# A layernorm, linear-attention and gated-MLP kernel: 96 bytes less padding, and another order of the opening

## The chip, the cores and the metric

The kernel runs on one core of a Trainium2 chip. A core has five engines that work side by side, each with its own queue of instructions in order: TensorE (PE, matrix products into PSUM), VectorE (DVE, elementwise work and reductions), ScalarE (ACT, copies and activation functions), GpSimd (POOL, elementwise work on SBUF) and SyncE (SP, which here issues nearly all DMAs). SBUF is the working memory of 128 partitions, PSUM the eight banks of 128 x 512 float32 into which PE writes. The metric is the time of one execution on the device in microseconds (us).

## The reference

All inputs are float32. `x` is 2048 x 1024.

```python
xn = layernorm(x)                       # over the 1024 columns, eps 1e-5
q, k, v = split_heads(xn @ wqkv)        # 32 heads of 32
phi(t) = concat(softmax(t @ w_phi), softmax(-(t @ w_phi)))      # per head
num = phi(q) @ (phi(k)^T @ v);  den = phi(q) @ sum(phi(k)) + 1e-6
s = merge_heads(num / den) @ wo
g = silu( (silu(xn @ w1) * (xn @ w3)) @ w2 )                    # w1, w3: 1024 x 3584
out = x + s * g
```

## The kernel before

**Products.** Each float32 operand is split into two float32r parts, a rounded one ("hi", a cast on ACT) and the rest ("lo", a subtraction on DVE). A product of two operands takes three passes of matmuls: hi x hi, hi x lo, lo x hi. On top of that the large products use Strassen's scheme with seven products of half size: A's halves give A11, A12, S1, S2, S3, S4, A22, the weights' halves B11, B21, T1, T2, T3, B22, T4. What the text calls *a product* is one of these seven for one block: 4 x 3 = 12 matmuls of 128 x 128 (stationary) by 128 x 512 (moving) into one PSUM bank (`products`, L703). Bank `a` takes A12; bank `c` S1, then S4; a bank `b` (four of them) A11, then S2, S3 and A22 on top. `out_of` (`evict`) takes the sum out of the bank behind each product; the next one that adds to the same bank waits for that.

**Stages.** (1) Layernorm of x and the transposes of it. (2) Gate and up (w1, w3): 2 halves of x (`tb`) x 28 column blocks x 7 products = 392 products of L703; the stationary operand is a weight block `bo` (a tile of the pool `q`), the moving one a tile `op0...` (first half of x) or, behind *the turn*, `op1...` (second half). (3) k, v and q (L927): 3 passes over 8 pairs of row tiles, 7 products each; stationary `xo...` (pool `q`), moving the weight tiles `op2...`, `op3...`, `op4...`. (4) w2 (L1333): 7 x 8 rounds of 7 blocks of 6 matmuls; stationary `af`/`as`, moving `bo` from a ring of 24 tiles (`ring`: 8 of pool `ra`, 12 of `rb`, 4 of `rw`). (5) The attention output times wo (L1460), stationary `oT` (pool `q`), moving `wos` (the same ring).

**Where tiles lie.** Pools are stacked from the left end of a partition (`edge_l`, `misc`, `small`, `work`, `q`, `big`; later `acc` and `rb` in the place of `big`) and from the right end (`edge_r`, `rw`, `bdp`, `xp`; later `spare` and then `ra` in the place of `bdp` and `xp`). `edge_l`, `edge_r` and the tile `pad` in `small` hold nothing; their sizes shift what is stacked behind them. `op0...` tiles are all in `big`. Of `op1...`, A11 and A12 are in `spare`; of `op2...`, T2 and T1; of `op3...`, T3 and B22; of `op4...` none (`HOMES`). In this program `small` ends at byte 5216 of the partition, 96 past a multiple of 512; all sizes behind it up to `big` are multiples of 512, so all these tiles start 96 past one. `big` ends at 179,296, `spare` starts at 179,712 = 351 x 512, and every tile of the right side but the edge starts on a multiple of 512.

**The opening.** Everything up to the 14th product is written out by hand, and each engine keeps that order. Tiles x0 to x3 are normalized, turned (`turn`: four transposes on PE into a PSUM tile `pt` of the tag `tr`, two buffers), copied out (`raw_x`, ACT) and cast (`hi`, ACT): one such pair of ACT instructions is *a piece*; there are four for A11 and four for A12. Tiles x4 to x7 follow (`nm_scalar` is the shift and scale on ACT; `other_turns`, two turns each, A22's, copied out by ACT, and A21's, read by DVE in `first_sums`, which makes S1 and S3). The sums S2 (`second_sums`) and S4 (`last_sums`) are DVE's. `b_first` to `b_third` make the weights' sums on POOL; `hold_sums` is a small copy on POOL that keeps it back until a given tile is written. `finish_h0` is a SiLU on ACT, for blocks 2 and 3 with a store to `hs_d`.

**Folds.** 32 weight blocks of q and k are multiplied by the block diagonal of w_phi (`fold`, eight PE instructions for one, into `tr`), copied back (`copy_fold`, ACT) and stored. Six of them are done in the opening (`load_fold` loads two into one `q` tile), the other 26 in the main loop (`side_fold`), every sixth step from the main loop's first on.

Of the kernel before, what the change touches and what calls it, by code (L numbers as in the profile page):

```python
# [8 lines left out]
F = mybir.dt.float32  # L9
# [8 lines left out]
P = 128  # L18
# [3 lines left out]
G = 8  # L22
NKB = NF // 4
EPS = 1e-5
PAD = 32


@with_exitstack
def tile_kernel(ctx: ExitStack, tc: tile.TileContext, x, wkT, wqT, wv, wphi, wo, w1, w3, w2, out):
# [3 lines left out]
    def pool(name, bufs, **kw):  # L33

        open_pools[name] = tc.tile_pool(name=name, bufs=bufs, reuse_waits="tile", **kw)
        return open_pools[name].__enter__()
# [108 lines left out]
    ps = pool("ps2", 2, space=PSUM)  # L145
    BANKS = {"a": 1, "b": 4, "c": 1}
# [7 lines left out]
    def slot(m, j):  # L154
        name = f"op{m}" + (ANAMES if m < 2 else BNAMES)[j]
        j = HOMES[m][j]
        if j < 7:
            return big.tile([P, 2, 4, 512], R, name=name, tag=f"big{j}")
        return spare.tile([P, 2, 4, 512], R, name=name, tag=f"spare{j}")
# [12 lines left out]
    def quad(name, dt=R):  # L172
        return qp.tile([P, 2, 4, P], dt, name=name, tag="q")

    def blk(name):
        return xp.tile([P, 4, P], F, name=name, tag="x")

    def flat(t):
        return t.rearrange("p k t -> p (k t)")
# [3 lines left out]
    eps_t = consts[:, 0:1]  # L183
    small.tile([P, PAD], F, name="pad", bufs=1)
    bd = bdp.tile([P, G, P], F, name="bd")
# [32 lines left out]
        for a in range(2):  # L218
            nc.vector.tensor_scalar(xt[a], xt[a], mv[:, j, 0:1], sd[:, 1, j:j + 1], op0=OP.subtract, op1=OP.mult)

    def turn(half):
        pt = ps.tile([P, 4, P], F, name="pt", tag="tr", bufs=2)
        for k in range(4):
            nc.tensor.transpose(pt[:, k, :], half[:, k * P:(k + 1) * P], ident)  # L224
        return pt

    def raw_x(pt):
        xf = blk("xf")
        nc.scalar.copy(xf, pt)
        return xf  # L230
# [13 lines left out]
    def load_w(wT, dch, c, t=None):  # L244
        wr = blk("wr") if t is None else t
        nc.sync.dma_start(wr, wT[dch][:, 4 * c:4 * c + 4])
        return wr

    def fold(wr, c):

        pw = ps.tile([P, 4, P], F, name="pw", tag="tr", bufs=2)
        for g in range(4):
            nc.tensor.matmul(pw[:, g, :], wr[:, g], bd[:, 4 * c + g, :], start=True, stop=True)  # L253
        return pw
# [9 lines left out]
    ao, bos, xs = {n: slot(0, j) for j, n in enumerate(ANAMES[:5])}, {}, []  # L264
# [46 lines left out]
    def place(n, q, u):  # L311
        return ao[n][:, u, :, q * P:(q + 1) * P]

    def raw_at(n, q):
        return raw[q][n]

    def hi(n, *qs):
        for q in qs:
            nc.scalar.copy(place(n, q, 0), raw_at(n, q))

    def lo(n, *qs):
        for q in qs:
            nc.vector.tensor_sub(place(n, q, 1), raw_at(n, q), place(n, q, 0).bitcast(F))  # L323
# [4 lines left out]
    def raw_b(k, n):  # L328

        if n in ("B11", "B21") and k < 4:  # L330
            return early_b(k, n)
        r = raw_of(k)
        t2 = t2b[0] if k == 1 else wk[4]
        return {"B11": r["B11"], "B21": r["B21"], "T2": t2, "T1": r["B11"], "T3": r["B12"], "B22": r["B22"], "T4": r["B21"]}[n]

    def bhi(k, n):
        if (k, n) not in bos:
            bos[k, n] = quad("bo")
        nc.scalar.copy(bos[k, n][:, 0], raw_b(k, n).rearrange("p (k n) -> p k n", n=P))  # L339

    def blo(k, n):
        b = bos[k, n]
        nc.vector.tensor_sub(b[:, 1], raw_b(k, n).rearrange("p (k n) -> p k n", n=P), b[:, 0].bitcast(F))  # L343
# [14 lines left out]
    raw = [{} for _ in range(4)]  # L358
# [18 lines left out]
    def nm_scalar(t):  # L377

        g, j = group(t)
        for a in range(2):  # L380
            nc.scalar.activation(xs[t][a], xs[t][a], AF.Identity, bias=shift[:, t:t + 1], scale=sds[g][:, 1, j:j + 1])

    def hold_sums(ap):

        nc.gpsimd.tensor_copy(consts[:, 1:2], ap)

    def first_half(n, *qs):

        for q in qs:
            raw[q][n] = raw_x(turn(xs[q][n == "A12"]))  # L390
            hi(n, q)

    def other_turns(q):

        raw[q]["A22"] = raw_x(turn(xs[4 + q][1]))
        return turn(xs[4 + q][0])

    def first_sums(q, pt):
        for j, n in enumerate(("S1", "S3")):
            raw[q][n] = s_room[:, j, q].rearrange("p (k t) -> p k t", k=4)  # L400
        nc.vector.tensor_add(raw[q]["S1"], pt, raw[q]["A22"])
        nc.vector.tensor_sub(raw[q]["S3"], raw[q]["A11"], pt)
# [8 lines left out]
            nc.vector.tensor_sub(raw[q]["A12"], raw[q]["A12"], raw[q]["S2"])  # L411
            raw[q]["S4"] = raw[q]["A12"]

    at_fold, OPEN_FOLDS = 0, 6
    folded, t2b = [], []

    def load_fold():
        nonlocal at_fold
        t = quad("wr", F)
        for u in range(2):  # L420
            folded.append((at_fold, load_w(*folds[at_fold][:3], t[:, u])))
            at_fold += 1

    def copy_fold(f):
        m, wr, pw = f
        nc.scalar.copy(wr, pw)
        nc.sync.dma_start(folds[m][3], flat(wr))

    def next_fold():
        m, wr = folded.pop(0)  # L430
        return m, wr, fold(wr, folds[m][2])
# [180 lines left out]
    banks, acts = {}, {}  # L612
# [79 lines left out]
    def products(step):  # L692

        k, an = seq[step]
        tb = k // NF
        b = BANK[an]
        if an in ("A11", "A12", "S1"):
            banks[k, b] = ps.tile([P, 512], F, name=f"bank{b}", bufs=BANKS[b])
        bank, bt = banks[k, b], bos.pop((k, OPERAND[an]))
        n = 0  # L700
        for kk in range(4):
            for u, w in PASSES:
                nc.tensor.matmul(bank, bt[:, w, kk], aos[tb][an][:, u, kk], start=an in ("A11", "A12", "S1") and n == 0,  # L703
                                 stop=LAST[b] == an and n == 11, skip_group_check=True)
                n += 1

    def out_of(step):
        k, an = seq[step]
        evict(step, k, an, banks[k, BANK[an]])

    def finish_h0(k):
        nc.scalar.activation(h0_early.get(k, h0s[k % 2]), h0_early.get(k, h0s[k % 2]), AF.Silu)
        if k in h0_early:
            nc.sync.dma_start(hs_d[k - 2], h0_early[k])
# [7 lines left out]
    nm(0)  # L722
    bhi(0, "B11")
    nm_scalar(1)
    first_half("A11", 0)
    st(3)
    sds[1] = root(mvs[1])
    first_half("A12", 0)
    rstd(mvs[1], sds[1])
    nm(2)  # L730
    nm(3)
    first_half("A11", 1)
    first_half("A12", 1)
    blo(0, "B11")
    lo("A11", 0, 1)
    first_half("A11", 2, 3)
    lo("A11", 2, 3)
    bhi(1, "B11")
    first_half("A12", 2, 3)
    products(0)  # L740
    lo("A12", 0, 1)
    blo(1, "B11")
    products(1)
    bhi(0, "B21")
    bhi(1, "B21")
    bhi(2, "B11")
    lo("A12", 2, 3)
    blo(0, "B21")
    products(2)
    blo(1, "B21")  # L750
    blo(2, "B11")
    hold_sums(bos[2, "B11"][:, 1, 0, 0:1].bitcast(F))
    b_first(0)
    b_second(0)
    b_third(0)
# [29 lines left out]
    products(5)  # L785
    load_fold()
    load_fold()
    pt = other_turns(0)
    t2b.append(quad("t2", F).rearrange("p u k t -> p (u k t)")[:, :512])
    hold_sums(xs[7][1][:, 0:1])  # L790
    b_first(1)
    b_second(1)
    b_third(1)
    first_sums(0, pt)
    pt = other_turns(1)
    out_of(5)
    finish_h0(0)
    first_sums(1, pt)
    products(6)
    pt = other_turns(2)  # L800
    finish_h0(1)
    out_of(6)
    first_sums(2, pt)
    products(7)
    pt = other_turns(3)
    hi("S1", 0, 1, 2)
    first_sums(3, pt)
    hi("S1", 3)
    bhi(0, "T1")
    finish_h0(2)  # L810
    lo("S1", 0, 1, 2, 3)
    blo(0, "T1")
    f0, f1 = next_fold(), next_fold()
    out_of(7)
    copy_fold(f0)
    copy_fold(f1)
    b_load(2, rws[0], "B11")
    products(8)
    second_sums()
    f2 = next_fold()  # L820
    hi("S2", 0, 1, 2, 3)
    lo("S2", 0, 1, 2, 3)
    bhi(0, "T2")
    blo(0, "T2")
    out_of(8)
    products(9)
    finish_h0(3)
    copy_fold(f2)
    hi("S3", 0, 1, 2, 3)
    out_of(9)  # L830
    f3 = next_fold()
    lo("S3", 0, 1, 2, 3)
    bhi(0, "T3")
    blo(0, "T3")
    products(10)
    copy_fold(f3)
    b_load(2, rws[0], "B12")
    bhi(1, "T2")
    blo(1, "T2")
# [6 lines left out]
    lo("A22", 2, 3)  # L846
    blo(0, "T4")
    b_load(2, rws[0], "B21")
    f4 = next_fold()
    products(12)  # L850
    last_sums()
    ao["S4"] = slot(0, 5)
    hi("S4", 0, 1, 2, 3)
    bhi(0, "B22")
    copy_fold(f4)
    lo("S4", 0, 1, 2, 3)
    blo(0, "B22")
    b_load(2, rws[0], "B22")
    bhi(1, "T1")
    f5 = next_fold()  # L860
    products(13)
    blo(1, "T1")
    out_of(12)
    b_first(2)
    bhi(1, "T3")
    blo(1, "T3")
    copy_fold(f5)
    out_of(13)
    out_of(11)
    bhi(1, "B22")  # L870
    blo(1, "B22")

# [235 lines left out]
    bos = {}  # L1108
# [53 lines left out]
    ps = pool("ps", 2, space=PSUM)  # L1162
    BANKS = {"a": 2, "b": 3, "c": 2}
# [187 lines left out]
    old, banks, first, second, eager = None, {}, ready[0], None, ExitStack()  # L1351
    for r, new in enumerate(steps):
# [16 lines left out]
        bank = {}  # L1369
# [69 lines left out]
        old, banks = new, bank  # L1439
# [5 lines left out]
    ps = pool("ps4", 2, space=PSUM)  # L1445
# [149 lines left out]
```

## Time and profile before

| | us |
|---|---|
| median of three runs | 2388.03 (2385.86 to 2388.47) |
| the profiled execution | 2386.34 |
| its span, first to last instruction | 2384.3 |
| start of product 0 on PE | 19.59 |
| start of product 8 (S1 of block 0), all matmuls but the first | 51.79 |
| start of the main loop's first product on PE | 76.95 |
| the turn to the second half of x | about 600 |
| k, v, q stage | about 1140 to 1630 |
| w2 stage | 1635 to 2180 |
| last stage | 2180 to the end |

The page of the profile gives each engine's busy time, the chain of work that ended last (followed back from the last instruction to what released it) and the costliest groups of instructions. The chain in order of time has one piece per line: start, length, engine, output and line of the kernel, and how many instructions in a row. A timeline has, per line: start, time from the first one's start to the last one's end, engine, line, operation, output<-inputs, shapes, count, and in brackets the idle time ahead of it and what ended that. Matmuls are pipelined: the shown duration of one (0.39) overlaps the next, so the pace is read from starts. A windows view gives busy time and instructions of each engine in a stretch of time, then the granted TensorE clock and the DMA's share and rate.

### The profile page before, as it was taken

The page shows a single profiled execution, that of the slowest core. Times are in us where ns is not written, and L with a number is a line of the kernel's source. Part 1 is how long each engine was busy: PE and PEld are TensorE (multiplying, and loading weights), DVE is VectorE, ACT ScalarE, POOL GpSimd, SP SyncE. Part 2 cuts the span into 40 slices and gives each one's busy share as a digit, 9 for nine tenths or more (in the row PEclk, how much of TensorE's full clock was granted, in tenths as well). Part 3 has the DMA queues.
Part 4 walks back from the last instruction along what each step waited for, and adds up shares of the span by engine and source line. Part 5 has one row for each costly group of instructions (what it writes and reads, how often), then busy time and mean ns, then how long its engine had stood idle before and what let it go on. Part 6 is the DMA issues. An engine that isn't in the chain of part 4 may idle for free.

```text
span 2384.3 us, 35860 instructions
## 1 busy us (share of the span) xinstructions
PE 2355.8 (99%) x13298; PEld 1924.5 (81%) x13298; DVE 1750.9 (73%) x2531; ACT 861.3 (36%) x1535; POOL 759.1 (32%) x571
## 2 busy tenths in 40 slices
PE   7999999999999999999999999999999999999999
PEld 5788888888788888888888788888888888887777
DVE  7767887774688878885566555788678778778883
ACT  6554544543344444443221111334423222243110
POOL 2333545442355555552000000230011111115872
PEclk9999999999999999999999999999999999999999
DMA  5667699987877787776998867999444443367753
GB/s 179 195 212 250 217 332 332 311 294 223 252 276 257 246 278 274 260 255 228 363 341 333 324 228 280 351 352 307 153 140 147 177 177 131 108 252 285 249 185 126
DMA packets 320558, 588.93 MB, mean 247 GB/s; under 512 B 25728, under 2 KB 158336, under 8 KB 317696
## 3 DMA queue, kind: packets, MB, share of 16 engines
q1 hardware_dynamic: 305600, 571.96, 69.1%
q10 hardware_dynamic: 14784, 14.68, 1.8%
q8 instruction: 105, 1.72, 0.3%
q14 instruction: 69, 0.57, 0.1%
HBM read 380.76 MB, written 206.32 MB: 246 GB/s over the span
## 4 chain that ended last, share of the span: by engine, by line
PE 94%; DVE 2%; DMA 1%; ACT 1%; SPq 1%; issue 1%; POOL 0%; DVEq 0%; ACTq 0%
PE bankb L703 23%; PE bankb L1333 13%; PE bankc L703 12%; PE bankb L927 11%; PE pm L1460 7%; PE bankc L1333 7%; PE banka L703 6%; PE bankc L927 6%; PE banka L1333 3%; PE banka L927 3%; PE po L1304 1%; PE pkv L912 1%; PE pw L253 1%; DVE bo L343 1%; PE pt L224 0%
## 5 line engine op out<-in xcount | busy, mean ns | idle before, releaser
L343 DVE TENSOR_TENSOR bo<-rw,bo 128x512 fp32r<-128x512 f32 x332 | 307.1, 926 | 155.1 <-ACT bo L339 154.6
L1343 POOL TENSOR_TENSOR acc<-acc,u 128x512 f32<-128x512 f32 x48 | 63.5, 1323 | 459.8 <-ACT u L1342 445.0
L1333 PE MATMUL bankb<-bo,as 128*128 128x512 f32 x816 | 204.0, 393 | 0.0
L339 ACT CAST bo<-rw 128x512 fp32r<-128x512 f32 x332 | 199.0, 617 | 6.7 <-DMA rw<-in_w 4.0
L1333 PEld LDWEIGHTS bankb<-bo,as 128*128 128x128 f32 x816 | 153.2, 188 | 35.0
L1460 PE MATMUL pm<-wos,oT 128*128 128x512 f32 x720 | 168.7, 393 | 0.0
L703 PE MATMUL bankc<-op0S,bo 128*128 128x512 f32 x672 | 163.8, 392 | 2.7 <-DVE bo L343 1.8
L703 PE MATMUL bankb<-op0S,bo 128*128 128x512 f32 x672 | 163.6, 392 | 2.4 <-DVE bo L343 1.6
L703 PE MATMUL bankb<-op1A,bo 128*128 128x512 f32 x672 | 163.8, 393 | 0.0
L703 PE MATMUL bankb<-op0A,bo 128*128 128x512 f32 x672 | 163.6, 392 | 0.0
L703 PE MATMUL bankb<-op1S,bo 128*128 128x512 f32 x672 | 161.9, 390 | 1.2 <-ACT h L643 1.2
L703 PE MATMUL bankc<-op1S,bo 128*128 128x512 f32 x672 | 161.9, 390 | 1.0 <-ACT bo L339 1.0
L1460 PEld LDWEIGHTS pm<-wos,oT 128*128 128x128 f32 x720 | 134.6, 188 | 32.5 <-issue 2.9
L703 PEld LDWEIGHTS bankb<-op1S,bo 128*128 128x128 f32 x672 | 126.1, 188 | 28.6 <-ACT h L643 1.6
L703 PEld LDWEIGHTS bankc<-op1S,bo 128*128 128x128 f32 x672 | 126.1, 188 | 28.4 <-ACT bo L339 1.4
L703 PEld LDWEIGHTS bankc<-op0S,bo 128*128 128x128 f32 x672 | 125.1, 188 | 29.5 <-DVE bo L343 2.4
L703 PEld LDWEIGHTS bankb<-op1A,bo 128*128 128x128 f32 x672 | 126.3, 188 | 28.0
L1333 PE MATMUL bankc<-bo,as 128*128 128x512 f32 x576 | 148.7, 393 | 0.0
L703 PEld LDWEIGHTS bankb<-op0S,bo 128*128 128x128 f32 x672 | 125.2, 188 | 29.0 <-DVE bo L343 2.2
L703 PEld LDWEIGHTS bankb<-op0A,bo 128*128 128x128 f32 x672 | 124.9, 188 | 26.2 <-DVE op0A L323 0.4
L1345 DVE TENSOR_TENSOR acc<-bankb,acc 128x512 f32<-128x512 f32 x152 | 104.5, 687 | 38.4 <-PE bankb L1333 35.5
L129 POOL TENSOR_TENSOR rw<-rw 128x512 f32<-128x512 f32 x56 | 82.0, 1464 | 156.2 <-DMA rw<-in_w 111.5
(262 smaller groups left out, 4717.1 us busy)
## 6 DMA issues: line engine op xcount, KB each, us to landing
rw<-in_w SPq DMA_DIRECT2D x224, 256.0 KB, 4.0
hr<-h_d SPq DMA_DIRECT2D x56, 512.0 KB, 3.7
xoS<-xo_d0S SPq DMA_DIRECT2D x48, 512.0 KB, 8.7
xoS<-xo_d1S SPq DMA_DIRECT2D x48, 512.0 KB, 6.4
xoA<-xo_d0A SPq DMA_DIRECT2D x36, 512.0 KB, 7.7
xoA<-xo_d1A SPq DMA_DIRECT2D x36, 512.0 KB, 6.3
e<-e_d SPq DMA_DIRECT2D x32, 512.0 KB, 5.7
h_d<-h SPq DMA_DIRECT2D x56, 256.0 KB, 4.4
```

The source lines that it names most:

```text
L129: nc.gpsimd.tensor_sub(b12, b22, b12)
L253: nc.tensor.matmul(pw[:, g, :], wr[:, g], bd[:, 4 * c + g, :], start=True, stop=True)
L339: nc.scalar.copy(bos[k, n][:, 0], raw_b(k, n).rearrange("p (k n) -> p k n", n=P))
L343: nc.vector.tensor_sub(b[:, 1], raw_b(k, n).rearrange("p (k n) -> p k n", n=P), b[:, 0].bitcast(F))
L703: nc.tensor.matmul(bank, bt[:, w, kk], aos[tb][an][:, u, kk], start=an in ("A11", "A12", "S1") and n == 0, stop=LAST[b] == an and n == 11, ...
L912: nc.tensor.matmul(pkv[sl, m], e[:, m // 4, (m % 4) * P + 32 * h:(m % 4) * P + 32 * h + 32], v[:, 4 * (m % 4) + h], start=first and m == 0 ...
L927: nc.tensor.matmul(bank[b], xo[an][:, u, k], wb[bn][:, w, k], start=an in ("A11", "A12", "S1") and n == 0, stop=LAST[b] == an and n == 11, ...
L1304: nc.tensor.matmul(po[a][32 * j:32 * j + 32, 256 * c:256 * c + 256], kvt[sl, c, j, s], ets[c, j // 2][sl, 2 * (j % 2) + s].rearrange("p t ...
L1333: nc.tensor.matmul(bank[b], t[:, u, pos + k], bos[kb, bn, k][:, w], start=first and n == 0, stop=LAST[b] == an and n == 5, skip_group_chec ...
L1343: nc.gpsimd.tensor_add(c, c, u)
L1345: nc.vector.tensor_add(c, pb, c)
L1460: nc.tensor.matmul(p, oT[a][k // 4][:, u, k % 4], wos[c, 4 * (k % 2) + k // 2][:, w], start=n == 0, stop=n == 23)
```

## The change

The tile `pad` shrinks from 32 to 8 floats (128 to 32 bytes a partition). Six folds in the opening become eight, with one more `load_fold`; the main loop then has 24. `turn` can put its result into the banks `a` and `c` as well; for that, `products` allocates its banks by the tags `bka`, `bkb`, `bkc`. In the opening, A11's four pieces come ahead of A12's on ACT and on PE, the root of the second pair of tiles ahead of all of them, and the third and fourth turn of each four use the banks `c` and `a`; the second and fourth pair of `other_turns` use bank `c`. PE turns pairs 0 and 1 ahead of product 6, pairs 2 and 3 ahead of product 7. Some casts, subtractions, `out_of(7)` and three `finish_h0` change places, and the folds are two behind products 7 and 8 each and one behind each of 9, 11, 12 and 13.

```diff
-PAD = 32
+PAD = 8
-    def turn(half):
-        pt = ps.tile([P, 4, P], F, name="pt", tag="tr", bufs=2)
+    def turn(half, b=None):
+
+        pt = ps.tile([P, 4, P], F, name="pt", tag=f"bk{b}" if b else "tr", bufs=BANKS[b] if b else 2)
...
-    at_fold, OPEN_FOLDS = 0, 6
+    at_fold, OPEN_FOLDS = 0, 8
...
-            banks[k, b] = ps.tile([P, 512], F, name=f"bank{b}", bufs=BANKS[b])
+            banks[k, b] = ps.tile([P, 512], F, name=f"bank{b}", tag=f"bk{b}", bufs=BANKS[b])
...
     nm_scalar(1)
-    first_half("A11", 0)
     st(3)
     sds[1] = root(mvs[1])
-    first_half("A12", 0)
+    first_half("A11", 0)
+    first_half("A11", 1)
     rstd(mvs[1], sds[1])
     nm(2)
     nm(3)
-    first_half("A11", 1)
+    first_half("A11", 2, "c")
+    first_half("A11", 3, "a")
+    bhi(1, "B11")
+    blo(0, "B11")
+    lo("A11", 0, 1, 2, 3)
+    first_half("A12", 0)
     first_half("A12", 1)
-    blo(0, "B11")
-    lo("A11", 0, 1)
-    first_half("A11", 2, 3)
-    lo("A11", 2, 3)
-    bhi(1, "B11")
-    first_half("A12", 2, 3)
+    first_half("A12", 2, "c")
+    first_half("A12", 3, "a")
     products(0)
+    blo(1, "B11")
     lo("A12", 0, 1)
-    blo(1, "B11")
     products(1)
     bhi(0, "B21")
+    bhi(2, "B11")
     bhi(1, "B21")
-    bhi(2, "B11")
     lo("A12", 2, 3)
     blo(0, "B21")
     products(2)
+    blo(2, "B11")
     blo(1, "B21")
-    blo(2, "B11")
-    hold_sums(bos[2, "B11"][:, 1, 0, 0:1].bitcast(F))
+    hold_sums(bos[1, "B21"][:, 1, 0, 0:1].bitcast(F))
...
     load_fold()
     load_fold()
-    pt = other_turns(0)
+    load_fold()
+    pt0 = other_turns(0)
...
-    first_sums(0, pt)
-    pt = other_turns(1)
+    pt1 = other_turns(1, "c")
+    first_sums(0, pt0)
     out_of(5)
     finish_h0(0)
-    first_sums(1, pt)
+    first_sums(1, pt1)
     products(6)
-    pt = other_turns(2)
-    finish_h0(1)
+    pt2 = other_turns(2)
+    pt3 = other_turns(3, "c")
     out_of(6)
-    first_sums(2, pt)
     products(7)
-    pt = other_turns(3)
-    hi("S1", 0, 1, 2)
-    first_sums(3, pt)
-    hi("S1", 3)
+    first_sums(2, pt2)
+    hi("S1", 0, 1)
+    first_sums(3, pt3)
+    hi("S1", 2, 3)
     bhi(0, "T1")
-    finish_h0(2)
     lo("S1", 0, 1, 2, 3)
     blo(0, "T1")
     f0, f1 = next_fold(), next_fold()
-    out_of(7)
...
     second_sums()
-    f2 = next_fold()
     hi("S2", 0, 1, 2, 3)
+    f0, f1 = next_fold(), next_fold()
+    bhi(0, "T2")
     lo("S2", 0, 1, 2, 3)
-    bhi(0, "T2")
     blo(0, "T2")
+    finish_h0(1)
+    copy_fold(f0)
     out_of(8)
+    copy_fold(f1)
     products(9)
+    out_of(7)
+    hi("S3", 0, 1, 2, 3)
+    bhi(0, "T3")
+    finish_h0(2)
     finish_h0(3)
-    copy_fold(f2)
-    hi("S3", 0, 1, 2, 3)
     out_of(9)
...
     lo("S3", 0, 1, 2, 3)
-    bhi(0, "T3")
     blo(0, "T3")
     products(10)
...
+    f0 = next_fold()
     out_of(13)
     out_of(11)
+    copy_fold(f0)
```

More of the change, by code (lines that the diff above doesn't have):

```diff
@@ L385, in hold_sums, with first_half, other_turns @@
         nc.gpsimd.tensor_copy(consts[:, 1:2], ap)
[L387 to L393, printed above, removed]
+    def first_half(n, q, b=None):
+        raw[q][n] = raw_x(turn(xs[q][n == "A12"], b))
+        hi(n, q)
+    def other_turns(q, b=None):
         raw[q]["A22"] = raw_x(turn(xs[4 + q][1]))
-        return turn(xs[4 + q][0])
+        return turn(xs[4 + q][0], b)
     def first_sums(q, pt):
@@ L819, in tile_kernel @@
     second_sums()
-    f2 = next_fold()
     hi("S2", 0, 1, 2, 3)
+    f0, f1 = next_fold(), next_fold()
+    bhi(0, "T2")
     lo("S2", 0, 1, 2, 3)
-    bhi(0, "T2")
     blo(0, "T2")
+    finish_h0(1)
+    copy_fold(f0)
     out_of(8)
+    copy_fold(f1)
     products(9)
+    out_of(7)
+    hi("S3", 0, 1, 2, 3)
+    bhi(0, "T3")
+    finish_h0(2)
     finish_h0(3)
-    copy_fold(f2)
-    hi("S3", 0, 1, 2, 3)
     out_of(9)
-    f3 = next_fold()
+    f0 = next_fold()
     lo("S3", 0, 1, 2, 3)
-    bhi(0, "T3")
     blo(0, "T3")
     products(10)
-    copy_fold(f3)
+    copy_fold(f0)
     b_load(2, rws[0], "B12")
@@ L848, in tile_kernel @@
     b_load(2, rws[0], "B21")
-    f4 = next_fold()
+    f0 = next_fold()
     products(12)
@@ L854, in tile_kernel @@
     bhi(0, "B22")
-    copy_fold(f4)
+    copy_fold(f0)
     lo("S4", 0, 1, 2, 3)
@@ L859, in tile_kernel @@
     bhi(1, "T1")
-    f5 = next_fold()
+    f0 = next_fold()
     products(13)
@@ L866, in tile_kernel @@
     blo(1, "T3")
-    copy_fold(f5)
+    copy_fold(f0)
+    f0 = next_fold()
     out_of(13)
     out_of(11)
+    copy_fold(f0)
     bhi(1, "B22")
```

## The prediction

> **What bounds the kernel now.** I read the page first (span, engines, chain that ended last), then the chain in order of time, then PE's timeline, then ScalarE's (ACT) and VectorE's (DVE) of the first 80 us.
>
> ```profile
> span 2384.3 us, 35860 instructions
> ...
> PE 2355.8 (99%) x13298; PEld 1924.5 (81%) x13298; DVE 1750.9 (73%) x2531; ACT 861.3 (36%) x1535; POOL 759.1 (32%) x571
> ...
> PE 94%; DVE 2%; DMA 1%; ACT 1%; SPq 1%; issue 1%; POOL 0%; DVEq 0%; ACTq 0%
> ```
>
> TensorE (PE) ends last nearly everywhere. So the time is the number of matmuls times the spacing between them, plus the few places where PE waits. The spacing is not one number. The chain, one repeating round of seven products early and one late (start, length, what):
>
> ```profile
> 559.60 5.44 PE bankb L703 x24
> 565.04 2.72 PE banka L703 x12
> ...
> 578.64 5.44 PE bankb L703 x24
> ...
> 638.90 5.54 PE bankb L703 x24
> 644.44 2.81 PE banka L703 x12
> ...
> 655.42 2.72 PE bankc L703 x12
> 658.14 5.54 PE bankb L703 x24
> ...
> 1171.96 2.80 PE bankb L927 x12
> ...
> 1518.65 5.44 PE bankb L927 x24
> ```
>
> A product is 12 matmuls. Early it takes 2.72 us (0.2267 each), a round 578.64 - 559.60 = 19.04. Late, the round takes 658.14 - 638.90 = 19.24: the products of `banka` and one of the two of `bankb` now take 2.81, the others still 2.72. What separates them is where the moving operand lies. Early, all of it is in `big`, allocated from the left. Late, `op1A11` and `op1A12` are in `spare`, allocated from the right. The stationary operand is a `q` tile, on the left, both times. By the allocation of this program, `work`, `q`, `big` (later `acc`, `rb`) start 96 bytes past a multiple of 512, everything on the right starts on one. `big` ends 416 bytes below `spare`, so distance explains nothing; the remainder does. The w2 stage repeats it, six matmuls a block; counting `ring` calls, the blocks at 1816.27 and 1819.06 stream from the right, the others from the left:
>
> ```profile
> 1816.27 1.57 PE L1333 MATMUL bankb<-bo,af 128*128 128x512 f32 x6
> 1817.67 1.55 PE L1333 MATMUL bankb<-bo,as 128*128 128x512 f32 x6
> 1819.06 1.56 PE L1333 MATMUL banka<-bo,af 128*128 128x512 f32 x6
> 1820.46 1.54 PE L1333 MATMUL bankc<-bo,as 128*128 128x512 f32 x6
> 1821.83 2.88 PE L1333 MATMUL bankb<-bo,as 128*128 128x512 f32 x12
> 1824.55 1.52 PE L1333 MATMUL bankc<-bo,as 128*128 128x512 f32 x6
> ```
>
> Read the starts, not the durations, which overlap: right 1.40; left behind it 1.39; right 1.40; left 1.37; then two left blocks in 2.72, 1.36 each. Unequal remainders cost 0.04 a block, and the next left block needs time to settle.
>
> **Part 1, PAD 32 to 8.** It takes 96 bytes out of `small`, so every left tile moves to a multiple of 512; the right ones lie there already. No instruction changes. After it, moving and stationary operand have the same remainder everywhere (0 and 0), where now most have 96 and 96 (2.72) and the rest 0 and 96 (2.81). I take it that the difference of the two addresses counts, as when the weight load of the next matmul and the stream of the present one meet in the same part of the memory: then 0 and 0 runs like 96 and 96. What that is worth:
> - gate/up stage behind the turn: 28 rounds x 0.20 = 5.6;
> - k/v/q stage (L927): two right-hand products in each of 16 pairs, 32 x (2.81 - 2.72), plus 0.01 each for settling = 3.2; its third pass, all on the left, shows no more than 2.72;
> - w2 stage (L1333): 50 of its 98 `ring` tiles lie right, 25 pairs x 8 row pairs = 200 blocks x 0.045 = 9.0, and some 118 left blocks behind one x 0.02 = 2.4;
> - last stage (L1460): 4 of the 16 `wos` tiles lie right, 192 matmuls x 0.007 = 1.4, settling 0.8.
>
> Sum **22.4 us**. The trace holds no long matmul with both operands on multiples of 512, so the price is bounded from both sides. It cannot gain much over 22.4, since no row shows a whole product under 2.72. At worst 2.81 belongs to any moving operand on a multiple of 512: then the other 7400 of 9840 long matmuls (820 products in all) go up by 0.0075, +55, less the 5 of settling: +50. The nearest rows with both on multiples of 512 are short ones, and lean my way: the transposes (`ident` lies at remainder 0; `xt` right, `x_room` left) take the same either way, so nothing is wrong with 0 and 0 as such.
>
> ```profile
> 46.35 0.45 PE pt L224 x4
> ...
> 102.64 0.44 PE pt L224 x4
> ```
>
> The Trainium skill, SBUF — State Buffer, section Who interferes with whom, says that PE reads the moving operand and the weights through two independent ports and that "PE and ACT never wait on anyone". By that, no placing changes a matmul, and Part 1 would be worth 0; 2.81 against 2.72 in the same bank speaks against it.
>
> **Part 2, ScalarE's order up to product 0.** From the timelines of ACT, then DVE, then PE:
>
> ```profile
> 12.46 0.56 ACT L229 COPY xf<-pt 128x512 f32<-128x512 f32 x1
> ...
> 13.58 0.29 ACT L201 ACTIVATE sd<-mv,consts 128x2 f32<-128x2 f32 x1
> ...
> 18.91 0.62 ACT L319 CAST op0A<-xf 128x512 fp32r<-128x512 f32 x1
> ...
> 21.70 0.63 ACT L319 CAST op0A<-xf 128x512 fp32r<-128x512 f32 x1
> ...
> 34.32 2.94 ACT L381 ACTIVATE x_room<-x_room,consts,sd 128x512 f32<-128x512 f32 x4 [1.45 <-DVE consts L375]
> ...
> 12.38 0.21 DVE L196 BATCH_NORM_AGGREGATE mv<-st 128x2 f32<-128x12 f32 x1
> ...
> 25.00 1.27 DVE L195 BATCH_NORM_STATS2 st<-x_room 128x6 f32<-128x512 f32 x2
> ...
> 10.84 1.94 PE L224 MATMUL pt<-ident,xt 128*128 128x128 f32 x8 [10.84 <-DVE xt L219]
> ```
>
> A piece (copy, cast) is 1.13 on ACT: from the cast at 18.91 to that at 21.70 lie two pieces and one cast of B11 (0.52). A11's fourth ends at 19.5 now. In the new order the root comes first (ready 12.6, done 12.8), and the four pieces of A11 end by 12.8 + 4 x 1.13 = 17.4, some 0.3 later for the third turn, whose norm waits on the root. That frees product 0 two us earlier on ACT, but all eight turns stand ahead of it on PE, 0.21 a transpose this early (1.94 for eight, the last one's drain in it), from 14.4 on: six x 0.85 = 5.1, so it starts at about 19.4 against 19.6. And it isn't what counts: A12's fourth piece still stands behind eight pieces, the root and one cast, 22.7 against 22.3; DVE's lo's follow it, then the stats at 25.00, and what hangs on these, up to the shift for which ACT waits until 34.32. **+0.35**, whatever PE does. The transposes in banks `a` and `c` wait for nothing (both are first used by a product 6 us later or more); `hold_sums` only holds POOL back to the new last cast.
>
> **Part 3, from product 6 to product 14.** PE's starts now, and what DVE and ACT need for four pieces:
>
> ```profile
> 37.77 0.66 PE L224 MATMUL pt<-ident,x_room 128*128 128x128 f32 x4 [0.40 <-ACT xf L229]
> 39.10 0.66 PE L224 MATMUL pt<-ident,x_room 128*128 128x128 f32 x4 [0.68 <-ACT xf L229]
> ...
> 46.19 1.03 PE L224 MATMUL pt<-ident,x_room 128*128 128x128 f32 x8
> ...
> 51.79 2.79 PE L703 MATMUL bankc<-op0S,bo 128*128 128x512 f32 x11 [1.23 <-DVE bo L343]
> ...
> 76.95 2.97 PE L703 MATMUL bankc<-op0S,bo 128*128 128x512 f32 x12 [0.88 <-DVE wk L655]
> ...
> 47.44 0.69 DVE L401 TENSOR_TENSOR s_room<-pt,xf 128x512 f32<-128x512 f32 x1 [2.54 <-ACT xf L229]
> ...
> 48.65 2.49 DVE L323 TENSOR_TENSOR op0S<-s_room,op0S 128x512 fp32r<-128x512 f32 x4
> ...
> 47.30 2.18 ACT L319 CAST op0S<-s_room 128x512 fp32r<-128x512 f32 x4
> ```
>
> Now the second `pt` of a pair waits until DVE has emptied the buffer before last (39.10), and the fourth pair is turned only behind product 7 (46.19), so S1's last raw piece is done at 48.1. With the second pair's transposes in `c`, product 6 starts at 39.05 (39.52 now), ends 41.8; pairs 3 and 4 follow at once, the last turn at 43.9; product 7 ends 46.6. S1's sums are done at 45.5, its four lo's (0.60 each) and T1's at 48.5, while PE does two folds (46.6 to 48.6). Product 8 runs 48.7 to 51.45; now it ends at about 54.4. Then S2: four sums and five lo's of 0.60 on DVE, 53.85, under two more folds; product 9 ends 56.5. Product 10 waits on ACT, which casts T2 till 51.95, then has a SiLU, two fold copies and bank `c`'s copy (four times 0.5: 54.0), four S3 casts (2.15), T3's (0.55), two SiLUs (1.05) and bank `b`'s copy, which must be out before S3 is added there: 58.3. It ends at 61.0. Products 11, 12, 13 with a fold behind each of 11, 12 and 13 end at 63.75, 67.45, 71.75 (13 waits 0.5 for DVE), and product 14 starts at 72.7, where it stood at 76.95: **-4.2**, the 0.35 of Part 2 included. Behind it operands and loads come by the same dependences, shifted as much. The two SiLUs moved behind product 9 take their stores to `hs_d` along on SP, behind two fold stores; they are read back at steps 18 and 20 only. The bounds: nothing (ACT late at each step) and -6.6, all that PE idles from 20 to 80:
>
> ```profile
> 20.00:80.00 60.00, 53.33 (x262) 42.66 (x261) 49.42 (x89) 37.86 (x70) 16.37 (x17) 1.00 0.33 108
> ```
>
> **Part 4, two more folds in the opening.** They leave the stream in which PE never waits. There, by the chain,
>
> ```profile
> 88.09 0.89 PE pw L253 x8
> 88.98 2.77 PE bankb L703 x12
> ```
>
> one costs 0.89, and 0.05 on the next product: **-1.9** for two. In the opening they fill waits; the one behind product 13 stands in the 0.9 us in which PE waits for bank `c`. Without that cover it would cost its 1.9 back. The fourth `wr` quad takes one of 11 `q` buffers until about 75; the next owners get buffers released 10 us earlier, so no cast waits. Its loads go out on SP ahead of stores that come 20 us later.
>
> **Sum.** -22.4 - 4.2 - 1.9 = -28.5. The profiled execution took 2386.34 (span 2384.3 and 2.0 around it), which gives 2357.8. The median of the three runs, 2388.03, is 1.7 above it, so I say **2359**.
>
> **Rivals.**
> - *Placing does nothing* (something other than the remainder sets 2.81, the pool's side itself, say): only the opening is left, 2388.0 - 6.1 = 2382. For it: no row shows 0 and 0 in a long matmul. Against: the sharp split.
> - *The other side: a moving operand on a multiple of 512 is slow in itself.* All long matmuls go to 2.81: 2388.0 + 50 - 6 = 2432. Nothing is then won back on the right, so it decides from 6.1 / 0.0075 = 800 slowed matmuls on, a ninth of the 7400. For it: every slow row has it. Against: the equal transposes.
> - *The opening's gain is eaten* (DVE, busy 49 of these 60 us, is the real limit, and runs late at each step): 2359 becomes 2363 to 2365.
>
> **How the numbers follow.** Forecast with its eaten opening 0.76 (own range 2352 to 2368), no effect 0.12, slow 0.10, 0.02 for anything else. The range 2352 to 2383 takes in the first two, about 0.83. A measurement tells 0.2% (4.8 us). The forecast is faster by 1.2%; the second case by 0.25%, so half of it counts as the same: faster 0.84, same 0.06, slower 0.10.
>
> **What would show it.** Right: late rounds of 19.04 like the early ones, w2 blocks of 1.36, product 14 near 72.7. Wrong: early products at 2.81 (the slow case), late ones still at 2.81 (no effect), product 14 at 76 or later (Part 3).

## The result and the profile after

| us | before | after |
|---|---|---|
| median | 2386.95 (2385.72 to 2388.47, 4 runs) | 2357.89 (2356.06 to 2360.53, 4 runs) |
| the profiled execution | 2386.34 | 2357.35 |
| its span | 2384.3 | 2355.2 |

The ratio is 0.988, with a 95% interval of 0.986 to 0.990: 29 us faster, where 2359 had been forecast. Repeated later beside other runs, the same kernel gave 2357.4 and 0.987 (0.9855 to 0.9888).

The page's first part after the change (busy time, share of the span and instructions of each engine):

```profile
PE 2330.3 (99%) x13298; PEld 1924.1 (82%) x13298; DVE 1755.1 (75%) x2531; ACT 861.2 (37%) x1535; POOL 759.4 (32%) x571
```

PE has the same 13298 matmuls, and is busy 25.5 us less with them (2355.8 - 2330.3). So most of the gain isn't waiting that went away; the matmuls follow each other more closely. PE's timeline behind the turn shows where, one round of seven products:

```profile
640.72 2.88 PE L703 MATMUL bankb<-op1S,bo 128*128 128x512 f32 x12
643.44 2.88 PE L703 MATMUL bankb<-op1A,bo 128*128 128x512 f32 x12
646.16 2.88 PE L703 MATMUL bankc<-op1S,bo 128*128 128x512 f32 x12
...
659.76 2.88 PE L703 MATMUL bankb<-op1S,bo 128*128 128x512 f32 x12
```

Read the starts: 2.72 from each to the next, also for the products that stream from the right-hand pool (`op1A`). The round takes 659.76 - 640.72 = 19.04; it took 19.24. In w2, six matmuls a block, left or right:

```profile
1788.65 1.52 PE L1338 MATMUL bankb<-bo,as 128*128 128x512 f32 x6
1790.01 1.52 PE L1338 MATMUL banka<-bo,af 128*128 128x512 f32 x6
```

1.36 from each to the next, as in the whole stage now; right-hand blocks took 1.40. The opening, from PE's timeline (the marks at the end are waits and what ended them):

```profile
39.20 3.02 PE L703 MATMUL banka<-op0A,bo 128*128 128x512 f32 x12
...
43.33 1.10 PE L225 MATMUL pt<-ident,x_room 128*128 128x128 f32 x8 [0.24 <-ACT xf L230]
...
48.70 3.11 PE L703 MATMUL bankc<-op0S,bo 128*128 128x512 f32 x12
...
54.42 2.79 PE L703 MATMUL bankb<-op0S,bo 128*128 128x512 f32 x11 [0.59 <-DVE bo L344]
...
58.68 5.74 PE L703 MATMUL bankb<-op0S,bo 128*128 128x512 f32 x24 [0.57 <-ACT wk L649]
...
73.35 2.96 PE L703 MATMUL bankc<-op0S,bo 128*128 128x512 f32 x12
```

Product 6 starts at 39.20, the last turn at 43.33, product 8 at 48.70 in one piece, product 9's rest at 54.42, product 10's at 58.68, product 14 at 73.35 without the wait of 0.88 ahead of it. Counted from the starts of PE's matmuls in both traces, stretch by stretch, the gain lies here:

| stretch on PE | before minus after, us | forecast |
|---|---|---|
| up to product 14 | 3.6 | 4.2 |
| products 14 to 196 (two folds fewer) | 2.3 | 1.9 |
| products 196 to 205 (the turn) | 2.95 | 0 |
| rest of gate/up | 5.2 | 5.6 |
| k, v, q | 2.5 | 3.2 |
| w2 | 10.3 | 11.4 |
| last stage | 2.2 | 2.2 |
| sum | 29.1 | 28.5 |

For gate/up, placing acts in three of these rows: the first right-hand products of the second half lie ahead of product 196 (0.19 gained from 176 on) and in the turn's row (about 0.2). With these, gate/up gained the 5.6 of the forecast, and 2.75 of the turn's row had no forecast.

Three things were left to settle: whether the placing works by what the prediction took (that the difference of the two addresses counts) or in some other way, what each part of the opening is worth, and the unforeseen 2.95 at the turn.

### The profile page after: what moved, and what is told of

Its sections match the earlier page's. It is cut to its first block, busy times and chain, and to the rows that moved or that the text cites. A ratio compares the mean times of both kernels' runs of the same rounds, so it can differ in the third digit from the quotient of the medians.

```text
span 2355.2 us, 35868 instructions
## 1 busy us (share of the span) xinstructions
PE 2330.3 (99%) x13298; PEld 1924.1 (82%) x13298; DVE 1755.1 (75%) x2531; ACT 861.2 (37%) x1535; POOL 759.4 (32%) x571
## 5 line engine op out<-in xcount | busy, mean ns | idle before, releaser
L1350 DVE TENSOR_TENSOR acc<-bankb,acc 128x512 f32<-128x512 f32 x152 | 104.3, 686 | 32.7 <-PE bankb L1338 28.6
```

The source lines that it names most:

```text
L1350: nc.vector.tensor_add(c, pb, c)
```

## The experiments

### 1. The new order with the old padding

```diff
-PAD = 8
+PAD = 32
```

> The changed kernel with PAD back at 32, so the left tiles lie 96 bytes past a multiple of 512 again and only the opening is new. Theory (the two addresses' difference sets the pace): rounds behind the turn 19.24 again, w2 blocks with right-hand tiles 1.40, product 14 still near 73.3, time 2358 + 22.4 to 24 = 2380 to 2382. Rival (the opening's order brought more than its 3.6 us, placing less): below 2376.

Measured: 2380.04 (2379.14 to 2382.99), against 2385.72 for the kernel before on the same chip; ratio 0.9978 (0.9968 to 0.9987). PE's timeline behind the turn:

```profile
652.26 2.97 PE L703 MATMUL bankb<-op1A,bo 128*128 128x512 f32 x12
655.07 2.90 PE L703 MATMUL bankb<-op1S,bo 128*128 128x512 f32 x12
657.80 2.97 PE L703 MATMUL banka<-op1A,bo 128*128 128x512 f32 x12
660.61 2.90 PE L703 MATMUL bankc<-op1S,bo 128*128 128x512 f32 x12
```

655.07 - 652.26 = 2.81 is back for the right-hand operands, and 660.61 - 657.80 too. The order alone is worth 5.7 us; the placing, on top of it, 2380.04 - 2357.89 = 22.2. (The second of these times is from other rounds; the kernel of experiment 3, which ran beside this one and has equal remainders too, took 2358.46, which makes it 21.6.)

### 2. The old order with the new padding

In the kernel before:

```diff
-PAD = 32
+PAD = 8
```

> The kernel before with PAD 8: only the placing is new. Theory: every round 19.04, every w2 block 1.36, product 14 at 76.9 as before, time 2387 - 22.4 = 2364.6, and 2361.6 if the 2.9 us that went at the turn came of the placing too. Rival: the turn's 2.9 belong to the new opening, so they are not in this run (2364 to 2365) but stay in the run with the new order and PAD 32.

Measured: 2362.87 (2362.44 to 2364.15), ratio 0.9903 (0.9888 to 0.9918). The placing alone is worth 2385.72 - 2362.87 = 22.9, and 5.7 + 22.9 = 28.6 is the whole change within its interval: the two parts add up. The opening stands as it did, with its wait of 0.88:

```profile
76.78 2.97 PE L703 MATMUL bankc<-op0S,bo 128*128 128x512 f32 x12 [0.88 <-DVE wk L655]
```

The waits at the turn, which the kernel before has and the changed one's profile has not, are there in this run. So the 2.95, but for the 0.2 said above, isn't a gain of the placing. By stages this run's trace gains 5.6 in gate/up (counted as above), 2.1 in k/v/q, 11.0 in w2 and 2.2 in the last stage on the kernel before, 20.9 in all. Another 1.8 come between products 14 and 155, where both operands of every product lie on the left in either kernel; 1.0 of that is a wait for a load in the trace of the kernel before, nearly gone in this one:

```profile
338.56 1.13 PE L253 MATMUL pw<-bd,wr 128*128 128x128 f32 x8 [1.12 <-DMA wr<-in_wqT]
```

### 3. Both sides on a remainder of 96

The changed kernel with the old padding, and the right end moved by the same 96 bytes:

```diff
-PAD = 8
+PAD = 32
...
-    edge[1].tile([P, 120], F, name="edge_r")
+    edge[1].tile([P, 96], F, name="edge_r")
```

> The changed kernel with PAD 32 and a right-hand edge 96 bytes smaller: both sides lie 96 bytes past a multiple of 512. Theory (only the difference of the addresses counts): as fast as the changed kernel, 2358, rounds of 19.04 everywhere. Rival (multiples of 512 count in themselves, the title's wording): products stay slow somewhere, 2370 or more; if any operand off a multiple of 512 were slow, the early products would be too.

Measured: 2358.46 (2358.02 to 2362.04), ratio 0.9887 (0.9872 to 0.9902), the changed kernel's own time. The same products, none on a multiple of 512:

```profile
650.76 2.88 PE L703 MATMUL bankb<-op1A,bo 128*128 128x512 f32 x12
653.48 2.88 PE L703 MATMUL bankb<-op1S,bo 128*128 128x512 f32 x12
656.20 2.88 PE L703 MATMUL banka<-op1A,bo 128*128 128x512 f32 x12
658.92 2.88 PE L703 MATMUL bankc<-op1S,bo 128*128 128x512 f32 x12
```

2.72 throughout. A multiple of 512 bytes is good for nothing in itself: what counts is that moving and stationary operand have the same remainder.

### 4. The price of a matmul against both addresses

A kernel of its own, in place of the whole computation; `W` and `M` start on multiples of 512, s and m are bytes:

```python
for u, w in ((0, 0), (0, 1), (1, 0)):
    a = s // 4 + 512 * w + P * kk
    b = m // 4 + 2048 * u + 512 * kk
    nc.tensor.matmul(p, W[:, a:a + P], M[:, b:b + 512], start=n == 0, stop=n == 47)
```

> A kernel of matmul streams alone, 43 blocks of 48, each with the product's three passes, stationary operand s and moving operand m bytes past a multiple of 512; it computes nothing of the reference. Theory: 0.2267 from start to start wherever s = m (0 and 0, 16 and 16, 96 and 96, 256 and 256), 0.2338 at s 96, m 0; what other differences do is open. Rival 1 (multiples of 512 in themselves): 96 and 96 differs from 0 and 0. Rival 2 (a shorter period): 0 and 256, or 0 and 128, run like 0 and 0. If some difference runs nearer to 512 columns at one a cycle (0.2133), the kernel can be made faster by it.

Measured, from the starts of consecutive blocks of 48 in PE's timeline (names: s and the stationary operand's remainder, m and the moving one's, in bytes):

```profile
45.02 11.37 PE L56 MATMUL s0m32x<-M,W 128*128 128x512 f32 x48
56.22 11.16 PE L56 MATMUL s0m64x<-M,W 128*128 128x512 f32 x48
67.22 11.37 PE L56 MATMUL s0m96x<-M,W 128*128 128x512 f32 x48
...
123.25 11.05 PE L56 MATMUL s0m256x<-M,W 128*128 128x512 f32 x48
134.14 11.37 PE L56 MATMUL s0m288x<-M,W 128*128 128x512 f32 x48
...
246.00 11.07 PE L56 MATMUL s96m96x<-M,W 128*128 128x512 f32 x48
256.91 11.37 PE L56 MATMUL s96m128x<-M,W 128*128 128x512 f32 x48
```

(56.22 - 45.02) / 48 = 0.2333 for a difference of 32, (67.22 - 56.22) / 48 = 0.2292 for 64, (134.14 - 123.25) / 48 = 0.2269 for 256, (256.91 - 246.00) / 48 = 0.2273 for 96 and 96. All cases:

| moving minus stationary, bytes | us of one matmul |
|---|---|
| 0 (0/0, 96/96, 256/256) | 0.2267, 0.2272, 0.2275 |
| 256 (0/256, 96/352, 256/0) | 0.2268 to 0.2275 |
| 64 and 320 | 0.2291 |
| the other multiples of 32 | 0.2331 to 0.2341 |
| 0, both at 16 | 0.2331 |
| 16 (0/16) and -16 (16/0) | 0.2316, 0.2333 |

The difference decides, but with a period of 256 bytes, not 512; 128 is as slow as 32. At 64 it costs only 0.0025, at other multiples of 32 some 0.007 as in the kernel. And a remainder of 16 is slow even where both operands have it: equal remainders are not always enough. No difference runs faster than 0.2267, so there is nothing left to gain here for this kernel.

### 5. A smaller weight load

The same kernel with c stationary columns:

```diff
-                    nc.tensor.matmul(p, W[:, a:a + P], M[:, b:b + 512], start=n == 0, stop=n == 47)
+                    nc.tensor.matmul(p[:c], W[:, a:a + c], M[:, b:b + 512], start=n == 0, stop=n == 47)
```

> Matmul streams alone again; it computes nothing of the reference. First the stationary operand is cut to 64 and 32 columns at differences of 0, 96 and 32 bytes, then both operands lie at the same remainder of 16 to 224, then at equal remainders of 256 or 64 apart. Theory (the next matmul's weight load is what the stream meets): at 96 the step over 0.2267 shrinks with the columns loaded, and may go altogether at 32. Rival (the stream itself is slow at such an address): it stays 0.2335 whatever is loaded. Equal remainders on multiples of 32 give 0.2267; 16 and 16 stays slow; 64 apart lies between (0.229).

```profile
44.40 11.37 PE L56 MATMUL c128s0m96x<-M,W 128*128 128x512 f32 x48
55.61 11.21 PE L56 MATMUL c64s0m0x<-M,W 128*64 128x512 f32 x48
66.65 11.27 PE L56 MATMUL c64s0m96x<-M,W 128*64 128x512 f32 x48
...
111.17 11.04 PE L56 MATMUL c32s0m32x<-M,W 128*32 128x512 f32 x48
122.05 11.25 PE L56 MATMUL c128s16m16x<-M,W 128*128 128x512 f32 x48
```

This is PE's timeline again; c is the number of stationary columns. With 128 columns a difference of 0 gives 0.2267 and 96 gives (55.61 - 44.40) / 48 = 0.2336. With 64 columns, (66.65 - 55.61) / 48 = 0.2300 at a difference of 0 and 0.2314 at 96. With 32, by the same reckoning, 0.2317 at 0, 0.2332 at 96, and (122.05 - 111.17) / 48 = 0.2267 at 32. That the step shrinks with the columns loaded fell: a fourth of the columns costs as much. What changes is which difference is free; with 64 columns none of the three that were tried is (0.2312 at 32). So the stationary operand's size has a part in it (besides the load, only the number of output rows differs between these cases), but the picture of one load meeting one stream in one part of the memory doesn't predict these numbers, and why 256, 64 and 16 are as they are stays open. Equal remainders of 32, 64, 128, 160, 192 and 224 all took 0.2271 to 0.2276, while 16 and 48 took 0.2311 and 0.2301. (16 and 16 had taken 0.2331 in experiment 4, so such a case also differs by 0.002 between the two runs.)

### 6. The old order up to product 2

The changed kernel with Part 2 undone:

```diff
+    first_half("A11", 0)
     st(3)
     sds[1] = root(mvs[1])
-    first_half("A11", 0)
-    first_half("A11", 1)
+    first_half("A12", 0)
     rstd(mvs[1], sds[1])
...
-    first_half("A11", 2, "c")
-    first_half("A11", 3, "a")
-    bhi(1, "B11")
-    blo(0, "B11")
-    lo("A11", 0, 1, 2, 3)
-    first_half("A12", 0)
+    first_half("A11", 1)
     first_half("A12", 1)
-    first_half("A12", 2, "c")
-    first_half("A12", 3, "a")
+    blo(0, "B11")
+    lo("A11", 0, 1)
...
```

> The changed kernel with the part up to product 2 in the order of before (A11 and A12 piece by piece, transposes in the two tr buffers alone). Theory: that part of the change costs, the stats of x4 at 25.0 instead of 25.56, so product 14 starts 0.4 to 0.6 earlier, near 72.8. Rival (A11's pieces ahead are what brings the opening's 3.6): product 14 at 75 or later.

Measured: 2355.96, one run, against 2386.04. PE's timeline has product 14 at

```profile
72.64 1.62 PE L703 MATMUL bankc<-op0S,bo 128*128 128x512 f32 x6
```

0.71 earlier than with the change. The total is among the shortest single times (the changed kernel's own reached 2355.66), and 2 us under its median is less than a run tells; the trace's starts carry the verdict. DVE's timeline has the statistics on which all that follows hangs at 24.82, where the changed kernel has them at 25.56:

```profile
24.82 1.28 DVE L195 BATCH_NORM_STATS2 st<-x_room 128x6 f32<-128x512 f32 x2
```

Putting the traces side by side, these statistics start at 25.00, 24.83 and 24.82 in the three executions with the old order (before and experiments 2 and 6), and at 25.56, 25.89, 26.14, 26.02, 26.33 and 25.83 in six with the new one (after and experiments 1, 3, 7, 8 and 10). Part of that spread is the arrival of x3. Counted from the start of x3's statistics, those of x4 start 14.52 or 14.53 later in all six with the new order, and 13.93, 13.51 and 13.57 later with the old. So Part 2 costs 0.6 to 1.0; between experiment 6 and the changed kernel, which differ in nothing else, it is 0.95.

### 7. Six folds in the opening

The changed kernel without its second fold behind product 8 and without the one behind product 13; the main loop has 26 again:

```diff
-    at_fold, OPEN_FOLDS = 0, 8
+    at_fold, OPEN_FOLDS = 0, 6
...
-    f0, f1 = next_fold(), next_fold()
+    f0 = next_fold()
...
-    copy_fold(f1)
...
-    f0 = next_fold()
     out_of(13)
     out_of(11)
-    copy_fold(f0)
```

> The changed kernel with six folds in the opening again (the second one behind product 8 and the one behind product 13 left to the main loop). Theory: both lie in waits, so product 14 stays at 73.3, and the two folds cost 1.9 later, between the 155th and the 176th product. Rival (they delay the opening): product 14 0.9 or 1.8 earlier, and nothing won by the eight.

Measured: 2360.47, one run. PE's timeline of the opening:

```profile
54.88 2.76 PE L703 MATMUL bankb<-op0S,bo 128*128 128x512 f32 x11 [1.34 <-DVE bo L344]
...
73.35 2.97 PE L703 MATMUL bankc<-op0S,bo 128*128 128x512 f32 x12 [0.88 <-DVE wk L655]
```

The two places from which the folds are gone are waits now, 1.34 and 0.88. Between products 155 and 176 this run gains only 0.12 on the kernel before, where the changed one gains 1.93: two folds are worth 1.8 there. Product 14 stands at the same 73.35, but x3's statistics on DVE had started 0.45 later in this execution. From there product 14 comes after 61.86, and after 62.31 with eight folds: they are not quite hidden, 0.45 comes back, behind product 9, where the second fold's copy makes ScalarE later for product 10 (its wait of 0.57 above; none here).

### 8. The old pairs of turns

```diff
-    pt1 = other_turns(1, "c")
     first_sums(0, pt0)
+    pt1 = other_turns(1)
...
     pt2 = other_turns(2)
-    pt3 = other_turns(3, "c")
     out_of(6)
-    products(7)
     first_sums(2, pt2)
+    products(7)
+    pt3 = other_turns(3)
```

> The changed kernel with the turns of x4 to x7 as before (pair 1 behind the first sums, pair 3 behind product 7, all in the two tr buffers). Theory: the turns ahead of products 6 and 7 carry most of the 3.6: product 8 two to four us later (51 to 52 instead of 48.7), product 14 at 75.5 to 77. Rival (the new order of casts and copies carries it): product 14 within 1 us of 73.35.

Measured: 2361.84, one run; product 14 at 79.15, beyond every theory's number. PE's timeline:

```profile
41.04 4.44 PE L703 MATMUL banka<-op0A,bo 128*128 128x512 f32 x12
45.32 1.03 PE L225 MATMUL pt<-ident,x_room 128*128 128x128 f32 x8
...
49.16 1.04 PE L225 MATMUL pt<-ident,x_room 128*128 128x128 f32 x8
...
79.15 2.97 PE L703 MATMUL bankc<-op0S,bo 128*128 128x512 f32 x12
```

The fourth pair is turned behind product 7 again, at 49.16. But something else is in these numbers. The windows view of the same run (busy time and instructions of PE, PE's loads, DVE, ACT, POOL; granted clock; DMA):

```profile
38.00:39.00 1.00, 0.00 (x0) 0.00 (x0) 0.73 (x2) 1.00 (x2) 0.74 (x2) 1.00 0.00 0
39.00:40.00 1.00, 0.66 (x4) 0.42 (x4) 0.89 (x2) 0.26 (x2) 1.00 (x1) 1.00 0.00 0
40.00:41.00 1.00, 0.54 (x4) 0.54 (x5) 0.39 (x1) 0.99 (x3) 0.92 (x1) 0.86 0.00 0
41.00:42.00 1.00, 1.00 (x4) 0.84 (x3) 0.51 (x1) 1.00 (x1) 0.92 (x2) 0.50 0.00 0
...
45.00:46.00 1.00, 1.00 (x10) 0.87 (x9) 0.49 (x1) 0.05 (x1) 0.00 (x0) 1.00 0.00 0
```

PE was busy 1.20 of the 3 us from 38 to 41 (2.33 in the kernel before), and the granted clock then fell to 0.50 until about 44. Product 6 took 45.32 - 41.04 = 4.28, where it takes 2.85 in the kernel before (39.52 to the next turn at 42.37): 1.43 lost. Counted from the start of x3's statistics on DVE (11.81 here, 11.04 after, 11.07 before), product 14 comes after 67.34 - 1.43 = 65.91, against 62.31 after and 65.88 before. So the turns' places are worth 3.6, as much as the whole opening gained, and 1.4 of this run's delay was the clock. That subtraction is worked out, not run again. The Trainium skill, TensorE: Matmul & The Clock Gate, section Part 1: The HAM clock gate, has PE's clock halved after an idle window of about 3.4 us and full again after about 3.4 us of work. The 0.50 and its length agree (the shares of the rows from 40 to 45 make 3.4 us of it); the idle window doesn't, since PE's longest wait here was 1.26. Nor is little work within 3 us enough by itself, as the kernel before shows behind product 8:

```profile
54.90:57.90 3.00, 1.16 (x8) 0.65 (x6) 2.86 (x5) 3.00 (x7) 0.00 (x0) 1.00 0.04 14
```

There PE was busy 1.16 of 3 us, and the clock stayed at 1.00 (in experiment 2 it did so with 1.15). What decides between the two isn't shown.

### 9. An earlier statistic

The trace of experiment 6 suggested a version that might beat all: its order, with the statistics of x4 moved to where DVE idles ahead of the second root.

```diff
     first_half("A12", 0)
+    st(4)
     rstd(mvs[1], sds[1])
...
     load_fold()
-    st(4)
     st(5)
```

> The run with the old pieces, and the stats of x4 (1.4 us on DVE) moved up from behind the weights' lo's to where DVE waits for the second root (12.6 to 13.9). Theory (DVE's row of stats and norms sets product 6 on): product 14 one us or more earlier than the 72.64 of the old pieces, near 71.5, bounded by product 5, which ends at 36; about 2 us under the changed kernel, less than a timing can tell. Rival (PE or ACT is late next): product 14 at 72.2 or later.

Measured: 2360.0 (2356.08 to 2366.33), ratio 0.9887 (0.987 to 0.9905): no better. On DVE's timeline

```profile
13.47 1.33 DVE L195 BATCH_NORM_STATS2 st<-x_room 128x6 f32<-128x512 f32 x2 [0.29 <-DMA x_room<-in_x]
```

the moved instruction first waits for its tile, and holds back the norms of x2 and x3 behind it, which start at 15.90 where they started at 14.71 in experiment 6. Product 14 comes at 74.15 instead of 72.64; 0.40 of that is x3's later arrival, 1.1 is the order. The idle time was no room for it.

### 10. The changed kernel again

> The changed kernel again, on the same chip and in the same rounds: 2357 to 2359, product 14 at 73.3; by the theory that the wait at the turn to the second half of x hangs on what the DMA queues reach in that stretch, not on the edit, it may show that wait (2 to 3 us) or not.

Measured: 2357.4 (2355.66 to 2358.84). Its profile differs from the first one of the same kernel most at the turn, where it gains 1.1 on the kernel before instead of 2.95. The windows view, before, after, and after again:

```profile
580.00:610.00 30.00, 28.83 (x127) 23.39 (x126) 9.14 (x13) 7.32 (x14) 5.59 (x5) 1.00 1.06 296
```

```profile
580.00:610.00 30.00, 30.00 (x134) 24.86 (x133) 13.35 (x17) 9.31 (x18) 6.79 (x5) 1.00 1.11 342
```

```profile
580.00:610.00 30.00, 28.83 (x126) 23.10 (x125) 12.29 (x16) 8.27 (x15) 6.48 (x5) 1.00 1.03 309
```

The last number is what the DMAs moved, in GB/s. PE works through these 30 us at 342 and waits 1.17 at 309 and at 296. In the other traces it goes the same way: no wait at 334 and 328 (experiments 6 and 8), a wait at 301, 304, 306, 317 and 319 (2, 3, 1, 7 and 9). The same kernel shows both, so the edit doesn't settle whether it comes. (Both traces with the whole old opening, before and experiment 2, have it; that the edit has no part in it isn't shown.) In the kernel before it stands twice, in PE's timeline:

```profile
609.92 3.01 PE L703 MATMUL bankb<-op1S,bo 128*128 128x512 f32 x12 [1.17 <-ACT h L643]
...
616.65 3.00 PE L703 MATMUL bankc<-op1S,bo 128*128 128x512 f32 x12 [1.00 <-ACT bo L339]
```

The chain of the kernel before leads back from there to a store on SP:

```profile
602.95 6.26 DMA h_d<-h
...
609.29 0.58 ACT h L643
```

ScalarE's copy into `h` has to wait until the store of the old `h` has landed. That store stands on SP behind four loads of `op1S`. Their issues took 6.1 us here (596.81 to 602.95), 6.65 in the repeated run (589.30 to 595.95) and 5.2 in the changed kernel's first trace (588.89 to 594.10). In these last two PE starts the product there at 602.46 and 602.64, but the copy at 601.82 and 600.23; the later one ends in the wait of 1.17, two products on. By this chain the wait comes from late transfers; the lower rate in the window may in part be its result. What makes the issues slower in one execution than in another wasn't tried.

## Why the prediction was right, and where it wasn't

**Part 1, the placing (22.4), was right** in its reason and nearly so in size: 21.6 or 22.2 by experiment 1, 22.9 by experiment 2. The step that carried it, "I take it that the difference of the two addresses counts", was the one no row could show; experiment 3 shows it for 96 and 96, experiment 4 over the whole range. By stages the sizes were 5.2 for 5.6, 2.5 for 3.2, 10.3 for 11.4 and 2.2 for 2.2 in the changed kernel's profile (experiment 2: 2.1 in k/v/q, 11.0 in w2); the 5.2 leaves out 0.4 ahead of product 205, so gate/up was right. That makes 20.6 to 20.9: k/v/q and w2 were priced too high by 1.5 to 1.8 together. That the medians come to 22 and 23 is partly luck, since one execution has waits that another hasn't, as in experiment 2. The picture given with it, the next matmul's weight load meeting the present one's stream, is only half supported: the columns loaded change which differences are free, but the cost doesn't shrink with them, and the period is 256 bytes. *Placing does nothing* falls with 2357.9 and with experiment 2; with it falls what was drawn there from the Trainium skill (SBUF — State Buffer, section Who interferes with whom), that independent read ports for the moving operand and the weights leave no room for placing: the two operands' remainders change the pace of these matmuls by 3% (0.2267 to 0.2336). That PE waited on another engine isn't shown by it. *A moving operand on a multiple of 512 is slow in itself* falls with every early product staying at 2.72.

**Part 2 (+0.35) had the right sign and a third to a half of the size (0.6 to 1.0).** The root was ready at 12.6 and the first piece began at 12.80, as forecast. The step that failed is "some 0.3 later for the third turn, whose norm waits on the root". ACT's timeline after the change:

```profile
12.60 0.29 ACT L201 ACTIVATE sd<-mv,consts 128x2 f32<-128x2 f32 x1 [0.30 <-DVE mv L196]
...
15.67 0.59 ACT L230 COPY xf<-pt 128x512 f32<-128x512 f32 x1 [0.52 <-PE pt L225]
...
22.49 0.62 ACT L320 CAST op0A<-xf 128x512 fp32r<-128x512 f32 x1
```

ACT waits 0.30 for the root's input and 0.52 for the third turn, and A12's fourth cast starts at 22.49, 0.79 later than before (21.70). The old order worked through pieces of the first two tiles while the other two were still loading and being normalized; the new one has nothing to put there. It passes on whatever delay x3's arrival has, as the constant 14.52 of experiment 6 shows; in the old order x4's statistics didn't come later where x3's did (11.07 and 25.00 before, 11.32 and 24.83 in experiment 2).

**Part 3 (-4.2) had the right mechanism**: the turns' places (experiment 8), product 6 at 39.20 for 39.05, the last turn at 43.33 for 43.9, product 8 at 48.70 for 48.7. From product 6 to product 14 the stretch fell from 76.95 - 39.52 = 37.43 to 73.35 - 39.20 = 34.15, by 3.3, where 3.8 was forecast. The term that was mis-sized is product 9's rest, 54.42 for 53.85, which waits for the last subtraction on DVE, and the rest follows: 58.68 for 58.3, 73.35 for 72.7. Counted from x4's statistics, behind which all of Part 3 lies, product 14 comes after 51.96 and 51.95 in the traces with the old opening (before, experiment 2), and after 47.79 to 47.82 with the new one, Part 2 left out or not (after, experiments 1, 3, 6 and 10): 4.15, where the forecast, its 0.35 for Part 2 taken out, has 4.55.

**Part 4 (-1.9) was right in the stream** (1.8 by experiment 7) and nearly so in its cover: behind product 13 the fold costs nothing, behind product 8 the second one costs 0.45. That was already in Part 3's list of what ACT does ahead of product 10 ("two fold copies"), so the sum didn't suffer; by its own account Part 4 is worth 1.4.

**What the prediction had not** is 2.75 of the 2.95 at the turn, waits of the profiled execution before. That the sum came out only 0.6 under what the profiles show is luck in part: these 2.75 and 0.2 more from products 14 to 196 made up for what was forecast too high in the opening, k/v/q and w2 (2.4). The medians come as near: 5.7 for the order and 22.9 for the placing make 28.6, against 28.5 forecast. *The opening's gain is eaten* was partly so (3.6 of 4.2).

## What to carry to other kernels

Where every matmul loads its own weights, look at the pace of long matmuls by pool: if the same shape runs at two paces, compare the remainders of the moving and the stationary operand's addresses, and make them equal by padding; a multiple of 512 is one way, a common multiple of 32 did as well in all cases tried. To price an opening that starts with loads, measure from the arrival on which it hangs, not from zero, since executions of one kernel differ there by more than an edit brings. An order that keeps an engine on data already present can be worth more than its instruction count says: 0.6 to 1.0 here, where 0.35 had been counted.

## What the runs showed of the hardware that was not expected

- The pace of a 128 x 128 by 128 x 512 float32r matmul with its own weight load depends on the difference of its operands' addresses with a period of 256 bytes: 0.2267 at 0, 0.2291 at 64, 0.2331 to 0.2341 at other multiples of 32. A common remainder of 16 or 48 is slow (0.2311 and 0.2331, 0.2301). With 32 columns loaded, 32 is the free difference (0.2267) and 0 isn't (0.2317).
- Behind three microseconds in which PE was busy 1.20, with no wait over 1.26, its granted clock fell to 0.50 for 3.4 us, which cost 1.43, in the middle of a kernel (experiment 8). The kernel before had 3 us with 1.16 busy and kept 1.00, so how little work it takes isn't settled.
- The same kernel ran through the turn without a wait in one execution, in which the DMAs moved 342 GB/s there, and with one of 1.17 in another, at 309; issuing the four loads ahead of the store on which it hung took 5.2 and 6.65 us (experiment 10).
